# Attention and a ReGLU feed-forward layer on one core: seven products in one more tile, the fourth product ahead of the sixth, later products with v, and merged last stores

## The chip, the core and the metric

The kernel runs on one core of one Trainium2 chip. The core has a matrix engine (TensorE, PE in the profile, with its weight loads shown as PEld), three engines that work on whole tiles (VectorE or DVE, ScalarE or ACT, GpSimd or POOL), a queue engine (SyncE, SP), and 16 DMA engines that they share. The metric is the device time of one execution in microseconds. The kernel before took 361.7 us, the median of three runs (361.11 to 362.02).

## The reference

```
scores = (1/8) * q @ k.T              # 8 batches, 8 heads, 576 rows, head size 64
scores = where(pos//64 >= pos.T//64, scores, -1e9)     # causal by blocks of 64
attn   = softmax(scores) @ v
x      = attn, heads side by side      # 4608 x 512
out    = (relu(x @ w_gate) * (x @ w_val)) @ w_out      # hidden size 1536, out 4608 x 512
```

Inputs and output are float32; the kernel multiplies in bf16 and accumulates in float32.

## The kernel before

**Tiles.** The rows of x are worked through in nine tiles j = 0 to 8 of 512 rows. Tile j < 8 is the first 512 rows of batch j. Tile 8 is made of the last 64 rows of each of the eight batches, the tails. The generator `ffn_gen` (L849) emits the feed-forward work of the tiles in order and yields after each piece, so that other work can be put between. For each tile it first emits 12 pairs of products, gate and val (f = 0 to 11, four 128x512 matmuls each, L855): ACT takes the relu of the gate (L865), DVE multiplies it with val into `hT` (L875). Then comes the product with `w_out`.

**The product with w_out, two ways.** In tiles 0, 1 and 2 it is 48 matmuls of 128x512 (L948), and DVE copies four results out (L958). In tiles from `SEVEN` on (L40, 3 before), `seven_products` (L759) treats each pair of hidden blocks and each half of the columns as a 2x2 block product and forms it from seven products instead of eight: 84 matmuls of 128x256 (L781). This needs sums and differences. Those of the weights are made once: `weight_sums` on POOL (W0 to W5, L684 and L687) and `weight_differences` on DVE, in place in `wo` (D0 to D5, twelve instructions, L698). Those of `hT` are made in each tile by the class `Sums`, twelve DVE instructions (L740): `step(f)` is called while the products of f run, and the last three instructions, `step(12)`, after the last `hT`.

The seven products are taken in the order 5 and 2 (into `y` and `z`), 1, 3 (into `y`), 6, 4 (into `z`), 7. Products 5 and 2 run first over the four hidden pairs that are ready early (`cs=range(4)`) and then over the last two, which need the sums of `step(12)`. Afterwards ACT copies `y` out (L812), DVE adds `z` (L813) and subtracts product 1 (L816); ACT copies `c12` out (L819), POOL makes `c22` (L822), DVE adds product 6 (L825); ACT copies `c21` out (L829), POOL adds it to `g` (L831) and DVE subtracts product 7 (L835; in tile 8 in two halves, L844). Outputs lie in four rotating buffers `ob`. `store_later` (L800) puts off each store until the next one is ready; so the store of a tile's `g` is issued in the next tile, right after its `c12` copy. ACT issues the stores; in tile 8 SP issues half of them.

**Attention rounds.** Beside tile b-1, the kernel does the attention of batch b in four rounds r = 4b to 4b+3 (two heads each). A round has a visit `s` (the products of q and k into a bank `one`, a bank `ffn` and two bank pairs `sc`, and the first exponentials), the last exponential `e`, the corners `c` (memsets of the masked blocks, on DVE at L1008 or POOL at L1011), the products with v of its two heads `a` and `b` (L586, L600, each followed on DVE by a reciprocal, a multiplication and, from batch 3 on, a small third instruction at L532), and `x`, a DMA transpose on SP that brings the rows to `xT` (L635), the operand of the next tile. After the last head of a batch another transpose (L572) brings the tail rows to `xTt`, for tile 8.

**What sets the order.** The order is written out by hand. `AT` (L1105) gives each piece a place on a scale of 144 pieces of feed-forward work per tile; `place_of` shortens the last 48 of them to 42 in tiles of seven products. The loop at its end takes the pieces by place and lets the generator run up to each. Each engine then works through its instructions in this order, waiting by semaphores; nothing overtakes. `HOW` says which engine or PSUM bank a piece uses: for a round, the engine of the corners and the banks of `a` and `b`. From batch 4 on, the last round of a batch uses `sc` for both and the others `one` and `ffn`. PSUM has two `sc` pairs, one `one` and three `ffn` banks; a matmul into a bank waits until its former content has been read.

Of the kernel before, what the change touches and what calls it, by code (L numbers as in the profile page):

```python
# [10 lines left out]
FP = mybir.dt.float32  # L11
BF = mybir.dt.bfloat16
AX = mybir.AluOpType
# [4 lines left out]
def kernel(  # L18
# [10 lines left out]
    nc = tc.nc  # L29

    B, H, S, D = q.shape
# [5 lines left out]


    FIRST = 3
    SEVEN = 3  # L40
    BASE = {0: 0, 1: 512, 3: 896, 2: 1024}
    AW = 1600
    TW = 256
# [9 lines left out]
    psum_ffn = ctx.enter_context(  # L53
        tc.tile_pool(name="psum_ffn", bufs=3, space=bass.MemoryType.PSUM)
    )
# [289 lines left out]
    def dma_transposes(b):  # L345
        m, tl = bfs[b, 0], bfs[b, 1]
        for t in range(2):
            nc.sync.dma_start_transpose(
                (qTm, kTm)[t][b % 2].rearrange("p c h n -> p (c h) n"),
                m[t],  # L350
            )
        tails_by_dma(b, tl)
# [305 lines left out]
    def put_block(j, hi, n0, ob, p0, p1):  # L658

        n = slice(n0, n0 + 256)  # L660
        rows = ob.rearrange("q (p n) -> q p n", n=256)
        if j < B:
            r0 = S * j + 256 * hi + 128 * p0
            nc.scalar.dma_start(
                out[r0 : r0 + 128 * (p1 - p0), n].rearrange("(p q) n -> q p n", q=128),
                rows,
            )
        else:
            for p in range(p0, p1):
                for i in range(2):  # L670
                    r0 = S * (4 * hi + 2 * p + i) + 512
                    (nc.scalar, nc.sync)[i].dma_start(
                        out[r0 : r0 + 64, n], rows[64 * i : 64 * i + 64, p - p0]
                    )

    sevens = []

# [81 lines left out]
    def seven_products(j, quads, sums):  # L759

        def times(to, which, p, c, first):
            two = wo[c // 2][:, 2 * (c % 2) : 2 * (c % 2) + 2, :]  # L770
            t = sevens[c // 2][:, 768 * (c % 2) : 768 * (c % 2) + 768]
            right = {
                5: two[:, 1, 256:512],
                2: two[:, 0, 0:256],
                1: t[:, 0:256],
                3: two[:, 0, 256:512],
                4: two[:, 1, 0:256],
                6: t[:, 256:512],
                7: t[:, 512:768],
            }[which]  # L780
            nc.tensor.matmul(  # L781
                to,
                sums.of(c)[which][:, 128 * p : 128 * p + 128],
                right,
                start=first,
                stop=(c == 5),
                skip_group_check=True,
            )

        def half(to, p):  # L790
            return to[:, 256 * p : 256 * p + 256]

        def whole(to, which, new=True, cs=range(6)):
            for p in range(2):
                for c in cs:
                    times(half(to, p), which, p, c, new and (p, c) == (0, 0))
                    if c % 2:
                        yield

        def store_later(hi, n0, ob, p0=0, p1=2):  # L800
            if store:
                store.pop()()
            store.append(lambda: put_block(j, hi, n0, ob, p0, p1))

        y = psum_ffn.tile([128, 512], FP, name="ffnp")
        z = psum_one.tile([128, 512], FP, name="one")
        for to, which in ((y, 5), (z, 2)):
            yield from whole(to, which, cs=range(4))
        for to, which in ((y, 5), (z, 2)):
            yield from whole(to, which, new=False, cs=(4, 5))  # L810
        g = sb.tile([128, 512], FP, name="ob", bufs=4)
        nc.scalar.copy(g, y)  # L812
        nc.vector.tensor_tensor(out=g, in0=z, in1=g, op=AX.add)  # L813
        m1 = psum_ffn.tile([128, 512], FP, name="ffnp")
        yield from whole(m1, 1)
        nc.vector.tensor_tensor(out=g, in0=m1, in1=g, op=AX.subtract)  # L816
        yield from whole(y, 3, new=False)
        c12 = sb.tile([128, 512], FP, name="ob", bufs=4)
        nc.scalar.copy(c12, y)  # L819
        store_later(0, 256, c12)  # L820
        c22 = sb.tile([128, 512], FP, name="ob", bufs=4)
        nc.gpsimd.tensor_tensor(out=c22, in0=g, in1=c12, op=AX.add)  # L822
        m6 = psum_ffn.tile([128, 512], FP, name="ffnp")
        yield from whole(m6, 6)
        nc.vector.tensor_tensor(out=c22, in0=m6, in1=c22, op=AX.add)  # L825
        store_later(1, 256, c22)
        yield from whole(z, 4, new=False)
        c21 = sb.tile([128, 512], FP, name="ob", bufs=4)
        nc.scalar.copy(c21, z)  # L829
        store_later(1, 0, c21)  # L830
        nc.gpsimd.tensor_tensor(out=g, in0=g, in1=c21, op=AX.add)  # L831
        if j < B:
            m7 = psum_ffn.tile([128, 512], FP, name="ffnp")
            yield from whole(m7, 7)
            nc.vector.tensor_tensor(out=g, in0=g, in1=m7, op=AX.subtract)  # L835
            store_later(0, 0, g)
        else:
            for p in range(2):
                m7 = psum_ffn.tile([128, 512], FP, name="ffnp")[:, 0:256]
                for c in range(6):  # L840
                    times(m7, 7, p, c, c == 0)
                    if c % 2:
                        yield
                nc.vector.tensor_tensor(  # L844
                    out=half(g, p), in0=half(g, p), in1=m7, op=AX.subtract
                )
                store_later(0, 0, half(g, p), p, p + 1)

    def ffn_gen():  # L849
        for j in range(B + 1):  # L850
# [27 lines left out]

            sums = Sums(quads) if j >= SEVEN else None

# [81 lines left out]

            if j >= SEVEN:
                sums.step(12)
# [40 lines left out]
    dve, act, pool = nc.vector.tensor_copy, nc.scalar.copy, nc.gpsimd.tensor_copy  # L1005
# [7 lines left out]
    with tc.manual_schedule(engines={E.PE, E.DVE, E.Activation, E.Pool, E.SP}):  # L1013
# [4 lines left out]
        def round_at(r, how):  # L1018

            exps = []  # L1020

            def begin():
                exps.extend(visit(r))
                exps[0]()
                exps[1]()

            corner, first, second, xT = how
            return {
                f"s{r}": begin,
                f"e{r}": lambda: exps[2](),  # L1030
                f"c{r}": lambda: corners(r, zeros_by[corner]),
                f"a{r}": lambda: head_av(r, 0, first),
                f"b{r}": lambda: head_av(r, 1, second),
                f"x{r}": lambda: (
                    to_xT_pe(r, by[xT[0]], xT[1]) if xT else to_xT_dma(r)
                ),
            }
# [58 lines left out]
        def mains_1(hp):  # L1096
# [8 lines left out]
        AT = {  # L1105
            "Lq0": -63.5,
            "Lq2": -62.27,
            "Lv0": -61.59,
            "Lv2": -59.5,
            "Lq6": -59.5,  # L1110
            "Lq4": -59.5,
            "v00": -58.48,
            "g00": -56.5,
# [214 lines left out]
            "x13": 377.61,  # L1328
            "a14": 378.59,
            "b14": 382.57,  # L1330
            "s15": 383.65,
            "e15": 383.74,
            "x14": 384.44,
            "c15": 388.17,
            "a15": 404.24,
            "b15": 404.37,
            "x15": 406.27,
        }
# [18 lines left out]
            "r11": ("dve", "one", "ffn", None),  # L1357
            "r12": ("dve", "ffn", "sc", None),
            "r13": ("dve", "sc", "ffn", None),
            "r14": ("dve", "sc", "ffn", None),  # L1360
            "r15": ("pool", "ffn", "ffn", None),
            "cv21/1": "dve",
            "cw21/1": "dve",
            "cv00/01": "dve",
# [114 lines left out]
        for b in range(4, B):  # L1479
            base = 144 * (b - 1)  # L1480
            for i in range(4):
                r = 4 * b + i
                here = ("sc", "sc") if i == 3 else ("one", "ffn")
                acts.update(round_at(r, ("dve", *here, None)))
                for n, p in STEADY.items():
                    AT[f"{n}{r}"] = base + 28 * i + p
            acts[f"L{b}"] = lambda b=b: last_keys(b)
            AT[f"L{b}"] = base + 11
            if b + 1 < B:
                acts[f"l{b + 1}"] = lambda b=b: load_qkv(b + 1, (0, 1), products[-1])  # L1490
                acts[f"lv{b + 1}"] = lambda b=b: load_qkv(b + 1, (2,))
                acts[f"d{b + 1}"] = lambda b=b: dma_transposes(b + 1)
                for n, p in (("l", 9), ("lv", 46), ("d", 66)):
                    AT[f"{n}{b + 1}"] = base + p
# [3 lines left out]
        )  # L1498
        for c in range(6):
            AT[f"W{c}"] = 232 + 3 * c  # L1500
            AT[f"D{c}"] = 436 + 5 * c

        assert set(acts) == set(AT), set(acts) ^ set(AT)

        def place_of(p):

            j, o = divmod(p, 144)
            if j < SEVEN:
                return p
            return 144 * SEVEN + 138 * (j - SEVEN) + min(o, 96) + max(0, o - 96) * 42 / 48  # L1510

# [35 lines left out]
```

## Time and profile before

| | |
|---|---|
| median of three runs | 361.7 us (361.11 to 362.02) |
| the profiled execution | 361.8 us |
| its span, first to last instruction | 360.0 us |
| mean granted TensorE clock | 0.997 |
| PE busy | 344.6 us |
| DVE, ACT, POOL busy | 202.5, 178.4, 138.8 us |
| tile 2: products of gate and val | 102 to 130 us |
| tile 2: product with w_out (48 matmuls) | 130.2 to 141.4 us |
| tiles 3 to 8: product with w_out | from 169.0, 206.9, 244.8, 283.9, 315.4 and 345.2 us |
| last matmul starts | 354.2 us |

A timeline line gives the start and the length of an instruction or of a run of equal ones, the engine, the line of the program, what it writes and reads, the shape, the count, and in brackets how long the engine was idle before it and what ended that. Matmul lengths overlap: a 128x512 matmul is listed at 0.38 us, but the next one starts 0.216 us later; a 128x256 one follows after 0.109 us, and one with v after 0.03 us. "ACTq" and "SPq" are the queue parts of those engines, which issue DMAs.

### The profile page before, as it was taken

What the parts mean: (1) busy time and instruction counts of PE and PEld (TensorE: products, weight loads), DVE (VectorE), ACT (ScalarE), POOL (GpSimd) and SP (SyncE); (2) the same over time, 40 slices, a digit from 0 to 9 for tenths busy, and PEclk for the clock granted to TensorE, in tenths of its full rate; (3) what the DMA queues carried; (4) which work ended last, traced back from release to release, by engine and by line L of the source; (5) the groups of instructions that cost most, each with busy time, mean ns of one, the idle gap of its engine ahead of it and who ended that gap; (6) DMA issues with size and microseconds to landing.
All of it is one profiled execution on the core that took longest, in us unless ns stands there. A gap on an engine that the chain in (4) does not pass through costs nothing.

```text
span 360.0 us, 7942 instructions
## 1 busy us (share of the span) xinstructions
PE 344.6 (96%) x3094; PEld 198.8 (55%) x3137; DVE 202.5 (56%) x510; ACT 178.4 (50%) x283; POOL 138.8 (39%) x181
## 2 busy tenths in 40 slices
PE   7899999999999999999999999999899999999993
PEld 3544455545545454555855585557555674484473
DVE  4663445678434454768446754766266745644661
ACT  4933666686336841665166625563555513323320
POOL 4647654697939600770269014830200020011002
PEclk9999999999999999999999999999999999999998
DMA  8999999999999994999479944998500240011005
GB/s 245 296 356 373 316 219 290 194 146 158 193 207 97 158 151 128 80 137 158 109 83 130 152 114 97 129 135 119 131 16 15 17 140 0 0 60 58 2 1 146
DMA packets 155077, 50.00 MB, mean 139 GB/s; under 512 B 134560, under 2 KB 150944, under 8 KB 155040
## 3 DMA queue, kind: packets, MB, share of 16 engines
q0 software_dynamic: 70480, 8.85, 45.5%
q1 hardware_dynamic: 76480, 31.47, 44.4%
q10 hardware_dynamic: 8080, 9.18, 8.2%
q8 instruction: 24, 0.39, 0.5%
q14 instruction: 13, 0.11, 0.1%
HBM read 37.75 MB, written 9.44 MB: 131 GB/s over the span
## 4 chain that ended last, share of the span: by engine, by line
PE 87%; ACT 5%; DVE 4%; issue 2%; POOLq 0%; POOL 0%; DVEq 0%
PE ffnp L855 49%; PE ffnp L781 10%; PE ffnp L948 8%; PE one L781 3%; PE sc L451 3%; PE one L451 2%; PE ffnp L586 2%; ACT attnT L415 2%; PE one L586 2%; ACT attnT L456 2%; PE sc L586 1%; PE one L855 1%; PE one L999 1%; DVE stage L740 1%; DVE hT L875 1%
## 5 line engine op out<-in xcount | busy, mean ns | idle before, releaser
L875 DVE TENSOR_TENSOR hT<-gate_sb,ffnp 128x512 bf16<-128x512 bf16 x106 | 72.6, 685 | 70.4 <-PE ffnp L855 46.1
L855 PE MATMUL ffnp<-xT,wv 128*128 128x512 bf16 x356 | 99.3, 379 | 2.3 <-DVE ob L835 0.7
L865 ACT ACTIVATE gate_sb<-ffnp 128x512 bf16<-128x512 f32 x103 | 62.2, 606 | 76.3 <-PE ffnp L855 71.6
L855 PE MATMUL ffnp<-xT,wg 128*128 128x512 bf16 x348 | 96.7, 380 | 1.3 <-DVE xT L630 0.3
L855 PEld LDWEIGHTS <-wv 128*128 128x128 bf16 x432 | 40.0, 98 | 46.4 <-issue 4.2
L855 PEld LDWEIGHTS <-wg 128*128 128x128 bf16 x432 | 39.7, 98 | 43.1 <-issue 3.1
L822 POOL TENSOR_TENSOR ob<-ob 128x512 f32<-128x512 f32 x6 | 7.6, 1262 | 133.8 <-ACT ob L819 118.5
L456 ACT ACTIVATE attnT<-sc 128x1024 bf16<-128x1024 f32 x56 | 57.3, 1043 | 0.0
L781 PEld LDWEIGHTS <-stage 128*128 128x128 bf16 x360 | 34.7, 98 | 5.2
L586 PEld LDWEIGHTS <-attnT 128*128 128x128 bf16 x640 | 26.3, 98 | 14.6 <-DVE attnT L1008 3.8
L948 PE MATMUL ffnp<-wo,hT 128*128 128x512 bf16 x137 | 33.3, 380 | 0.4
L740 DVE TENSOR_TENSOR stage<-hT 128x512 bf16<-128x512 bf16 (+2 forms) x72 | 33.0, 486 | 0.7
L463 ACT ACTIVATE attnT<-one 128x512 bf16<-128x512 f32 (+1 forms) x28 | 15.0, 536 | 30.5 <-PE ffnp L451 30.5
L339 POOL DMA_DIRECT2D q_bf<-in_q_dram x20 | 17.9, 911 | 27.5 <-DVE hT L875 23.3
L781 PE MATMUL ffnp<-stage 128*128 128x256 bf16 x216 | 26.5, 273 | 0.0
L339 POOL DMA_DIRECT2D v_bf<-in_v_dram x30 | 24.1, 854 | 4.0 <-PE ffnp L855 2.9
L948 PEld LDWEIGHTS <-hT 128*128 128x128 bf16 x144 | 13.3, 98 | 14.0 <-issue 0.6
L451 PEld LDWEIGHTS <-kTm 64*128 64x128 bf16 x384 | 13.1, 94 | 14.3 <-issue 8.3
L339 POOL DMA_DIRECT2D k_bf<-in_k_dram x20 | 17.7, 937 | 0.0
L451 PE MATMUL sc<-qTm,kTm 64*128 64x512 bf16 (+1 forms) x168 | 17.7, 305 | 0.0
L958 DVE COPY ob<-ffnp 128x512 f32<-128x512 f32 x12 | 8.3, 689 | 12.9 <-PE ffnp L948 12.8
L781 PEld LDWEIGHTS <-hT 128*128 128x128 bf16 x144 | 14.1, 98 | 1.6
(143 smaller groups left out, 444.0 us busy)
## 6 DMA issues: line engine op xcount, KB each, us to landing
out_dram<-ob ACTq DMA_DIRECT2D x32, 256.0 KB, 2.8
stage<-in_moe_w_val_dram SPq DMA_DIRECT2D x6, 512.0 KB, 8.2
stage<-in_moe_w_gate_dram SPq DMA_DIRECT2D x6, 512.0 KB, 8.6
stage<-in_moe_w_out_dram SPq DMA_DIRECT2D x6, 512.0 KB, 10.7
q_bf<-in_q_dram POOLq DMA_DIRECT2D x20, 128.0 KB, 4.6
k_bf<-in_k_dram POOLq DMA_DIRECT2D x20, 128.0 KB, 6.5
v_bf<-in_v_dram POOLq DMA_DIRECT2D x20, 128.0 KB, 6.1
stage<-in_v_dram SPq DMA_DIRECT2D x19, 128.0 KB, 5.4
```

Source lines behind the costliest of these rows:

```text
L339: ins = nc.gpsimd.dma_start(dst, part_of)
L451: nc.tensor.matmul(o, kTm[b % 2][head_of(hh), c, hp, :], qT, start=True, stop=True)
L456: return lambda: nc.scalar.activation(at[:, :, lo : lo + 512], sc, AF.Exp, scale=scale)
L463: nc.scalar.activation(at[:, hh, 1024 : 1024 + w], third[hh][:, 0:w], AF.Exp, scale=scale)
L586: nc.tensor.matmul(av[:, p, :], at[:, col : col + 128], v_bf[b % 2][:, c, h, :], start=(p == 0), stop=(c == p), skip_group_check=True,)
L740: nc.vector.tensor_tensor(out=out.rearrange("p (c n) -> p c n", c=m), in0=a, in1=b, op=op)
L781: nc.tensor.matmul(to, sums.of(c)[which][:, 128 * p : 128 * p + 128], right, start=first, stop=(c == 5), skip_group_check=True,)
L855: nc.tensor.matmul(to, (wg, wv)[t][f // 4][:, c, 128 * (f % 4) : 128 * (f % 4) + 128], x[:, c], start=(c == 0), stop=(c == 3),)
L865: nc.scalar.activation(gate_sb, gate, AF.Relu)
L875: nc.vector.tensor_tensor(out=h, in0=gate_sb, in1=val, op=AX.mult)
L948: nc.tensor.matmul(op, hT[f][:, 128 * s : 128 * (s + 1)], wo[f // 4][:, f % 4, n0:n1], start=(f == 0), stop=(f == 11),)
L958: nc.vector.tensor_copy(ob, op)
```

## The change

Five things are edited.

1. `SEVEN` becomes 2: tile 2 uses seven products as well. With it the twelve weight differences move from the start of tile 3 to the start of tile 2, and `place_of` shortens the last part of tile 2.
2. Product 4 is emitted ahead of product 6, with the copy of `c21` and POOL's addition that follow it; the store of `c12` comes behind the `c21` copy on ACT, and the store of `c22` behind that of `c21`.
3. In batches 4 to 7, `a`, `b` and `x` of the last round are put 5 places later.
4. Around tile 2, round 15's visit, exponential and corners come earlier (its visit 12 places), its `a` 4 places earlier. On PE the visit of round 15 now stands ahead of `b13`, `a14` and `b14`, directly behind `a13`. `a14` goes from bank `sc` to `ffn`, `a15` and `b15` from `ffn` to `sc`.
5. In tile 8 each store covers two batches at a time: SP and ACT issue five stores each instead of eight. The last two stay 64 KB each.

```diff
-    SEVEN = 3
+    SEVEN = 2
...
-            for p in range(p0, p1):
-                for i in range(2):
-                    r0 = S * (4 * hi + 2 * p + i) + 512
-                    (nc.scalar, nc.sync)[i].dma_start(
-                        out[r0 : r0 + 64, n], rows[64 * i : 64 * i + 64, p - p0]
-                    )
+            by_batch = out.rearrange("(b s) n -> b s n", b=B)
+            for i in range(2):
+                b0 = 4 * hi + 2 * p0 + i
+                (nc.scalar, nc.sync)[i].dma_start(
+                    by_batch[b0 : b0 + 2 * (p1 - p0) - 1 : 2, 512:576, n].rearrange(
+                        "b s n -> s b n"
+                    ),
+                    rows[64 * i : 64 * i + 64],
+                )
...
-        m6 = psum_ffn.tile([128, 512], FP, name="ffnp")
-        yield from whole(m6, 6)
-        nc.vector.tensor_tensor(out=c22, in0=m6, in1=c22, op=AX.add)
-        store_later(1, 256, c22)
         yield from whole(z, 4, new=False)
         c21 = sb.tile([128, 512], FP, name="ob", bufs=4)
         nc.scalar.copy(c21, z)
         store_later(1, 0, c21)
         nc.gpsimd.tensor_tensor(out=g, in0=g, in1=c21, op=AX.add)
+        m6 = psum_ffn.tile([128, 512], FP, name="ffnp")
+        yield from whole(m6, 6)
+        nc.vector.tensor_tensor(out=c22, in0=m6, in1=c22, op=AX.add)
+        store_later(1, 256, c22)
...
-            "s15": 383.65,
-            "e15": 383.74,
+            "s15": 371.65,
+            "e15": 376.74,
             "x14": 384.44,
-            "c15": 388.17,
-            "a15": 404.24,
+            "c15": 383.17,
+            "a15": 400.24,
...
-            "r14": ("dve", "sc", "ffn", None),
-            "r15": ("pool", "ffn", "ffn", None),
+            "r14": ("dve", "ffn", "ffn", None),
+            "r15": ("pool", "sc", "sc", None),
...
-                    AT[f"{n}{r}"] = base + 28 * i + p
+                    AT[f"{n}{r}"] = base + 28 * i + p + (5 if i == 3 and n in "abx" else 0)
...
-            AT[f"D{c}"] = 436 + 5 * c
+            AT[f"D{c}"] = 293 + 5 * c
```

## The prediction

> **What bounds the kernel.** I read the page first: PE is busy for nearly the whole span, and the chain that ended last lies on it.
>
> ```profile
> span 360.0 us, 7942 instructions
> ...
> PE 344.6 (96%) x3094; PEld 198.8 (55%) x3137; DVE 202.5 (56%) x510; ACT 178.4 (50%) x283; POOL 138.8 (39%) x181
> ...
> PE 87%; ACT 5%; DVE 4%; issue 2%; POOLq 0%; POOL 0%; DVEq 0%
> ```
>
> So a gain is a matmul less, a PE wait less, or a shorter end. After 60 us PE's timeline has waits of over 0.3 us in few places. Four times, in tiles 3 to 6, it waits inside the seven products. Tile 3, by the timeline:
>
> ```profile
> 169.86 1.04 PE L781 MATMUL one<-wo,stage 128*128 128x256 bf16 x8
> 169.97 0.96 DVE L740 TENSOR_TENSOR stage<-hT 128x512 bf16<-128x512 bf16 x3
> 171.02 0.31 DVE L1008 MEMSET attnT<- 64x128 uint32 x2
> 171.24 0.36 PEld L586 LDWEIGHTS <-attnT 128*128 128x128 bf16 x10 [0.63 <-DVE attnT L1008]
> ```
>
> PE has ended the first parts of products 5 and 2 (call this Z, 170.73) and meets `a`, whose corners queue on DVE behind all three sums of `step(12)`: 171.24 - 170.73 = 0.51 us. The second place is the end of tile 5:
>
> ```profile
> 251.68 1.71 ACTq L664 DMA_DIRECT2D out_dram<-ob  x2
> ...
> 255.62 0.58 ACT L829 COPY ob<-one 128x512 f32<-128x512 f32 x1 [3.35 <-PE ffnp L781]
> ...
> 256.25 0.27 PE L451 MATMUL one<-qTm,kTm 64*128 64x256 bf16 x1 [0.25 <-ACT ob L829]
> ...
> 257.63 0.69 DVE L835 TENSOR_TENSOR ob<-ob,ffnp 128x512 f32<-128x512 f32 x1 [3.25 <-PE ffnp L855]
> ...
> 258.37 0.38 PE L855 MATMUL ffnp<-xT,wv 128*128 128x512 bf16 x1 [0.75 <-DVE ob L835]
> ```
>
> The page blames PE for the `c21` copy's wait, but product 4 ended at 254.1. `c21` takes the buffer of the previous tile's `g`, whose store was issued at 251.68 and by the DMA view took 3.8 us to land (2.2 to 2.6 in the five other tiles). In that microsecond a 16 KB instruction fetch (queue q8) lay on a DMA engine. Price: the visit 0.3 late, val 0.9 late, 1.2 us.
>
> **The change, part by part**, on the profiled execution (361.8 us, 0.1 above the median; 1.8 of it lies around the span).
>
> *Tile 2, matmuls.* 48 x 0.216 = 10.37 us go, 84 x 0.1092 = 9.17 come: -1.2. The four DVE copies go and four additions of the same 0.69 us come; ACT gets three copies and POOL two additions, in windows where both idle.
>
> *Tile 2, DVE.* Twelve sums come (0.42 for 512 wide, 0.69 for 1024, 0.29 for 256) and the twelve weight differences, 0.2 apart. The latter find DVE idle between the `hT` of tile 2, and cost nothing; in tile 3, whose products took 0.2 us longer than tile 4's beside them, they are gone: -0.2. The sum after f = 4 falls ahead of the corners of `a12`, which PE awaits already at 114.35: the memsets end 0.34 later: +0.3.
>
> *Round 15's visit* is the costly part. It now comes three matmuls behind `a13`, and its second `sc` pair is the one that `a13` wrote; so it waits for DVE's last reading of `a13`. In the timeline before:
>
> ```profile
> 124.46 0.19 PE L600 MATMUL sc<-v_bf,attnL 128*128 128x65 bf16 x1
> ...
> 124.53 0.63 ACT L865 ACTIVATE gate_sb<-ffnp 128x512 bf16<-128x512 f32 x1
> 124.76 0.31 DVE L1008 MEMSET attnT<- 64x128 uint32 x2 [1.48 <-ACT attnT L456]
> 125.19 0.69 DVE L875 TENSOR_TENSOR hT<-gate_sb,ffnp 128x512 bf16<-128x512 bf16 x1
> 125.80 0.19 DVE L523 RECIPROCAL recip<-sc 128x5 f32<-128x5 f32 x1
> 126.02 0.42 DVE L525 TENSOR_TENSOR xnat<-sc,recip 128x256 bf16<-128x256 f32 x1
> 126.36 0.20 DVE L532 TENSOR_TENSOR xtail<-sc,recip 64x64 bf16<-64x64 f32 x1
> ```
>
> DVE has to do the corners of round 14 (after the exponential that ended at 124.67) and one `hT` (after the relu that ended at 125.16) first, so 126.57 is the earliest as before; a 512-wide sum now stands between them, +0.3: 126.87. PE reaches the pair at 124.49 + 3 x 0.216 + 0.09 + 0.45 (from a visit's start to its second pair, 129.19 to 129.64) = 125.69; with 0.2 from DVE's end to the matmul it starts at 127.1: +1.4 (1.1 without the sum). No bank of the kernel before showed this wait. Behind it queue on PE `b13`, gate and val of f = 10 and 11, `a14`, `b14`; `a14` waits for the `hT` of f = 10 (+0.1), and `b14`, now in the bank ring of `ffn`, for DVE's reading of `a14`, 1.0 us after that one's last matmul, where PE needs 0.9 from there: +0.3 with the load. Round 15's four exponentials on ACT now precede the relus of f = 10 and 11, which still end 0.2 and 0.9 us ahead of their val; its two POOL memsets and SP's transposes have microseconds to spare. The product with w_out then finds its sums: `step(12)`'s first ends 1.7 us after the start, needed at 1.86. Tile 2 together: -1.2 - 0.2 + 0.3 + 1.4 + 0.1 + 0.3 = **+0.7**.
>
> *Later products with v.* At Z PE now runs the last parts of 5 and 2 (0.87 us), which need only the first sum of `step(12)` (170.40), then two matmuls of product 1; `a` starts at Z + 1.09, after the corners (Z + 0.6). Four waits of 0.51 go: **-2.0**. On DVE the addition of `z` now precedes the readings of `a` and `b`; `b`'s ends at Z + 3.65 (before 3.3), and SP's transposes L572 and L635 behind it start at Z + 3.7 and 4.9. The next tile needs the last one at Z + 9.9 (10.4 before); landings there took 2.5 to 4.8, so it just holds.
>
> *Product 4 first.* `c21` could be copied 1.3 us earlier, but its buffer still waits for the `g` store, issued with the `c12` copy and 2.2 to 2.6 us on its way, against 2.8 when product 4 came second. Gain 0.2 to 0.5 of slack and no PE time. The `c12` store moves behind that copy, where ACT stood idle.
>
> *The fetch.* Page and trace give 24 fetches on q8, one per about 256 PE instructions (131 loads with their matmuls). Tile 2 gets 36 pairs more, so every later fetch falls 36 pairs earlier in the work: in tile 5 near Z + 2, ahead of the store: **-1.2**. In tile 6 it moves from Z + 7.9 to about Z + 3.5, onto L572. In tiles 3, 4 and 5 a transpose issue that met a fetch took 1.6 to 2.2 us instead of 1.2 and landed in up to 4.8; by tile 4's rows (2.3 to the next issue, 3.7 to landing) the row for tile 7 lands at Z + 9.7, needed at 9.0: **+0.6**. The Trainium skill ("Runtime: NRT & Kernel Launch", Instruction fetch mechanics) has a boundary of 16 KB cost one mostly hidden DMA step; by that the collision is none of the fetch's doing, the wait of tile 5 would stay, and the sum be 1.2 worse and, without tile 6's, 0.6 better.
>
> *The end.* Now two queues issue 16 stores of 64 KB for 0.5 to 0.6 us each:
>
> ```profile
> 351.21 5.80 SPq L672 DMA_DIRECT2D out_dram<-ob  x8
> ...
> 353.33 4.00 ACTq L672 DMA_DIRECT2D out_dram<-ob  x6
> ```
>
> The `c21` copy waits for tile 7's `g` store until 352.81, so it gains 0.3 (353.22 to 352.9), and the halves of `g` with it. Without the queueing the last issue moves from 356.78 to 356.05: -0.7 at best. Against it: ACT's `c12` half moves from 351.2 to 353.0, so 896 KB go out from 354 on, where now 768 KB took from 354.3 to 358.4, 185 GB/s with the DMA engines 80 to 90% busy: +0.4 at worst. I take **-0.2**, nearest the bandwidth rows. The Trainium skill ("DMA: Bandwidth & Descriptors", Rules for kernel authors) wants small transfers coalesced, and in the same table says that transfers to disjoint partition halves serialize on the same engines. By the first the end would be -0.7; the second stands with the trace.
>
> Sum: 361.8 + 0.7 - 2.0 - 1.2 + 0.6 - 0.2 = 359.7, **359.6 us** from the median.
>
> **Rivals.**
> - *A store or a fetch hits again* (0.20): the 1.2 us of tile 5 stay, or come in another tile. For: one in six tiles was hit; fetches jitter. Against: the moved places. 360.8.
> - *Tile 2 pays in full* (0.12): visit 15 and its followers don't wait. For: PE before had no such wait. Against: the same bank, and DVE's order. 359.6 - 2.1 = 357.5.
> - *Slower: the last transposes come late* (0.12). Each tile's last row block must land within about 4.9 us of its issue (4.0 in tile 6). In the products' stretches landings were 5.6 to 7.3; against it, loads run there, and behind Z none took over 4.8. At 6.0 us: 3 x 1.1 + 2.0, less the 0.6 already counted, is 4.7 more: 364.3. It turns the sign from 5.4 us on.
> - Mine (0.56): 359.6.
>
> **Numbers.** 0.3% (1.1 us) is about what a measurement here can tell from no change. Faster: mine and the full payment, 0.68 to 0.70; same: the second hit and part of the late transposes, 0.18; slower: 0.13. My own case runs from 358.3 (the end's -0.7, visit at 1.1, tile 6 unharmed) to 360.6; the range takes in the rivals next to it: 358.0 to 361.6.
>
> **What the trace after would show.** PE idle before visit 15's second `sc` pair, ended by DVE L532, about 1.4 us; no wait of PE on the corners in tiles 3 to 6; `c21` copies as soon as the `g` store has landed, not at product 4's end; no val late at tile 6's start, the gate of tile 7 on `xT` instead; ten stores at the end and the last matmul near 352.3. I am wrong if tile 3 starts before 141.5, if `a` still waits, or if gates wait for `xT` in tiles 4 to 6.

## The result, and the profile after

The changed kernel takes 359.5 us (median of 13 runs, 358.95 to 361.07), beside 362.85 us for the kernel before (13 runs, 361.04 to 365.8; the three behind the 361.7 us above are the first of them). The ratio is 0.991 (0.988 to 0.994). The profiled execution took 359.73 us, its span is 357.9 us, 2.1 us below that of before.

The page of the changed kernel: PE is still nearly always busy, and one instruction fetch more than before lies in the span (25 on q8, 24 before).

```profile
span 357.9 us, 8015 instructions
...
PE 342.8 (96%) x3131; PEld 202.0 (56%) x3173; DVE 207.5 (58%) x522; ACT 180.1 (50%) x286; POOL 141.2 (39%) x183
...
q8 instruction: 25, 0.41, 0.5%
...
PE 87%; DMA 5%; ACT 3%; POOL 1%; DVE 1%; issue 1%; POOLq 0%; SPq 0%; DVEq 0%; ACTq 0%
```

Lines of the program are three higher from the seven products on (L781 is now L784, L1008 is L1011). In what follows every span is cut into a start and three stretches by the times of PE's matmuls: A from tile 2's first gate matmul to tile 3's, B from there to the start of tile 8's seven products, C from there to the end of the span. Before: 101.86 + 39.60 + 203.70 + 14.85. After: 101.78 + 40.51 + 200.17 + 15.48. So in these two profiles tile 2 cost 0.9 us, the middle gained 3.5, and the end lost 0.6. Of the 0.9, only 0.5 belongs to the program; the rest is a wait that varies from execution to execution, as the experiments show.

**Tile 2.** The timeline after shows the predicted wait of round 15's visit: DVE's memset, sum and `hT` stand ahead of the reading of `a13`, and PE's second `sc` pair waits for L532.

```profile
125.31 0.31 DVE L1011 MEMSET attnT<- 64x128 uint32 x2 [1.49 <-ACT attnT L456]
125.63 0.42 DVE L743 TENSOR_TENSOR stage<-hT 128x512 bf16<-128x512 bf16 x1
...
125.97 0.68 DVE L878 TENSOR_TENSOR hT<-gate_sb,ffnp 128x512 bf16<-128x512 bf16 x1
...
126.02 0.38 PE L451 MATMUL sc<-qTm,kTm 64*128 64x512 bf16 x2
...
126.57 0.19 DVE L523 RECIPROCAL recip<-sc 128x5 f32<-128x5 f32 x1
...
126.79 0.42 DVE L525 TENSOR_TENSOR xnat<-sc,recip 128x256 bf16<-128x256 f32 x1
127.13 0.20 DVE L532 TENSOR_TENSOR xtail<-sc,recip 64x64 bf16<-64x64 f32 x1
...
127.40 0.39 PE L451 MATMUL sc<-qTm,kTm 64*128 64x384 bf16 x4 [0.99 <-DVE xtail L532]
```

**Tiles 3 to 6.** In the timeline of tile 3 PE goes from the first parts of products 5 and 2 into their last parts, then two matmuls of product 1, and `a` starts at 172.43 with no idle time in brackets: the memsets ended 0.5 us earlier.

```profile
171.34 0.60 PE L784 MATMUL ffnp<-wo,stage 128*128 128x256 bf16 x4
171.63 0.31 DVE L1011 MEMSET attnT<- 64x128 uint32 x2
171.78 0.60 PE L784 MATMUL one<-wo,stage 128*128 128x256 bf16 x4
...
172.22 0.38 PE L784 MATMUL ffnp<-stage 128*128 128x256 bf16 x2
...
172.43 0.47 PE L586 MATMUL sc<-v_bf,attnT 128*128 128x65 bf16 x10
```

Apart from single missing records, no gap of PE of over 0.2 us is left from tile 3's start to tile 8's seven products.

**The end.** Here is what I had not seen coming. In the timeline of tile 8 ACT's `c21` copy waits 2.97 us for a DMA:

```profile
347.95 0.59 ACT L822 COPY ob<-ffnp 128x512 f32<-128x512 f32 x1 [2.47 <-PE ffnp L784]
347.96 0.38 ACTq L664 DMA_DIRECT2D out_dram<-ob  x1
348.56 6.54 SPq L672 DMA_DIRECT2D out_dram<-ob  x5
...
351.50 0.58 ACT L828 COPY ob<-one 128x512 f32<-128x512 f32 x1 [2.97 <-DMA out_dram<-ob]
351.52 3.85 ACTq L672 DMA_DIRECT2D out_dram<-ob  x5
```

and the DMA view of 347 to 350 us has the cause: a fetch of 16 KB (at 348.63 in the DMA records) on top of `g`'s store, which took 3.4 us to land (2.2 before).

```profile
q8 instruction: 1, 0.02, 2.7%
issues: line engine op xcount, KB each, median us to landing
out_dram<-ob ACTq DMA_DIRECT2D x1, 256.0 KB, 3.4
```

### The profile page after: what moved, and what is told of

Its sections match the earlier page's. It is cut to its first block, busy times and chain, and to the rows that moved or that the text cites. A ratio compares the mean times of both kernels' runs of the same rounds, so it can differ in the third digit from the quotient of the medians.

```text
span 357.9 us, 8015 instructions
## 1 busy us (share of the span) xinstructions
PE 342.8 (96%) x3131; PEld 202.0 (56%) x3173; DVE 207.5 (58%) x522; ACT 180.1 (50%) x286; POOL 141.2 (39%) x183
## 4 chain that ended last, share of the span: by engine, by line
PE 87%; DMA 5%; ACT 3%; POOL 1%; DVE 1%; issue 1%; POOLq 0%; SPq 0%; DVEq 0%; ACTq 0%
PE ffnp L858 49%; PE ffnp L784 12%; PE ffnp L951 5%; PE one L784 5%; PE sc L451 3%; PE one L451 2%; PE ffnp L586 2%; DMA stage<-in_moe_w_gate_dram 2%; PE one L586 1%; DMA stage<-in_k_dram 1%; PE one L858 1%; PE sc L586 1%; PE ffnp L548 1%; ACT attnT L456 1%; DMA out_dram<-ob 1%
## 5 line engine op out<-in xcount | busy, mean ns | idle before, releaser
L825 POOL TENSOR_TENSOR ob<-ob 128x512 f32<-128x512 f32 x7 | 8.8, 1262 | 142.7 <-ACT ob L822 142.7
L784 PEld LDWEIGHTS <-stage 128*128 128x128 bf16 x420 | 40.4, 98 | 6.0
L743 DVE TENSOR_TENSOR stage<-hT 128x512 bf16<-128x512 bf16 (+2 forms) x84 | 38.5, 485 | 0.9
L784 PE MATMUL ffnp<-stage 128*128 128x256 bf16 x252 | 31.4, 273 | 0.0
L951 PE MATMUL ffnp<-wo,hT 128*128 128x512 bf16 x90 | 22.8, 379 | 0.3
L784 PEld LDWEIGHTS <-hT 128*128 128x128 bf16 x168 | 16.4, 98 | 1.9
L833 DVE TENSOR_TENSOR ob<-ffnp,ob 128x512 f32<-128x512 f32 x7 | 4.8, 692 | 21.6 <-POOL ob L825 15.0
L822 ACT COPY ob<-ffnp 128x512 f32<-128x512 f32 x7 | 4.1, 585 | 21.9 <-PE ffnp L784 21.9
```

What stands on the lines that cost most here:

```text
L743: nc.vector.tensor_tensor(out=out.rearrange("p (c n) -> p c n", c=m), in0=a, in1=b, op=op)
L784: nc.tensor.matmul(to, sums.of(c)[which][:, 128 * p : 128 * p + 128], right, start=first, stop=(c == 5), skip_group_check=True,)
L951: nc.tensor.matmul(op, hT[f][:, 128 * s : 128 * (s + 1)], wo[f // 4][:, f % 4, n0:n1], start=(f == 0), stop=(f == 11),)
```

## The experiments

Twelve kernels, in three groups of four; each group shared its runs of the kernel before (362.4, 362.4 and 362.6 us). Ratios are to those.

| kernel | median us | ratio (95%) | A | B | C |
|---|---|---|---|---|---|
| before | 362.4 to 362.85 | 1 | 39.60 | 203.70 | 14.85 |
| after | 359.5 | 0.991 (0.988-0.994) | 40.51 | 200.17 | 15.48 |
| after_again | 360.2 | 0.993 (0.991-0.996) | 40.74 | 200.16 | 15.59 |
| fetch_moved_after | 359.9 | 0.995 (0.992-0.997) | 41.51 | 200.17 | 14.34 |
| fetch_moved_before | 364.3 | 1.006 (1.004-1.008) | 39.70 | 204.11 | 14.83 |
| visit15_later | 360.0 | 0.994 (0.993-0.996) | 40.41 | 200.17 | 15.62 |
| v_later_alone | 362.0 | 1.000 (0.997-1.002) | 41.10 | 202.72 | 14.82 |
| fetch_tail | 359.15 | 0.990 (0.987-0.993) | 40.12 | 200.22 | 14.27 |
| order_6_4 | 360.3 | 0.995 (0.992-0.998) | 40.71 | 200.17 | 15.20 |
| fetch_tail_16_stores | 360.4 | 0.993 (0.990-0.996) | 40.11 | 200.19 | 15.71 |
| seven_from_tile_3 | 360.1 | 0.992 (0.989-0.995) | 41.35 | 202.17 | 14.28 |
| tails_transposed_later | 366.3 | 1.010 (1.007-1.013) | 47.32 | 200.29 | 15.18 |
| fetch_tail_6_4_in_tile_8 | 359.1 | 0.990 (0.987-0.992) | 40.60 | 200.18 | 14.50 |
| all_together | 365.3 | 1.008 (1.005-1.010) | 48.38 | 200.24 | 14.51 |

A, B and C are of the profiled execution. B repeats to 0.1 us wherever the program of the middle is the same; A does not, and with it the times of equal programs differ by about a microsecond.

What varies in A lies ahead of the last products of q and k of round 12 (L473): near 108 us PE waits for batch 3's transposed q and k, by up to 1.8 us more in one profile than in another. From there to tile 3's first gate, here before and after,

```profile
109.16 0.28 PE L473 MATMUL one<-qTt,kTt 128*128 128x64 bf16 x4
...
141.46 0.59 PE L855 MATMUL ffnp<-xT,wg 128*128 128x512 bf16 x2
```

```profile
109.49 0.28 PE L473 MATMUL one<-qTt,kTt 128*128 128x64 bf16 x4
...
142.29 0.59 PE L858 MATMUL ffnp<-xT,wg 128*128 128x512 bf16 x2
```

it takes 32.25 to 32.30 us in the four profiles whose tile 2 is that of before, and 32.79 to 32.81 in the eight whose tile 2 is that of the changed kernel. So the changed tile 2 costs 0.5 us, in every profile.

### Is it the fetch?

```diff
-            "j0": lambda: junk(7, 512),
+            "j0": lambda: junk(19, 192),
```

In the changed kernel:

> The changed kernel, with the seven 512-wide warm-up matmuls at the start cut into nineteen 192-wide ones: the same columns in a time in which PE waits for its first operands anyway, but twelve loads with twelve matmuls more, so that each later instruction fetch falls twelve pairs earlier in the work. In the changed kernel's profile a fetch at 348.63 us lay on the store of g in tile 8, which took 3.4 us to land instead of the 2.2 of before, and the c21 copy waited for it until 351.50. Fetch theory: the fetch of tile 8 starts 12 x 0.109 = 1.3 us earlier, the store lands in 2.2 to 2.5 us, the c21 copy starts 0.9 to 1.2 us earlier against the last matmul, and the time falls by 0.6 to 1.2 us against the changed kernel (359.5, so 358.3 to 358.9). Rival, the store is slow because SP's store of c12 goes out right behind it: the landing stays at 3.4 us and the time within 0.3 us.

C fell from 15.48 to 14.34 us; `g`'s store, issued at 349.18, let the `c21` copy start at 351.48, 2.3 us later. So the end gained what was expected. But the time did not fall: another fetch (107.10, before that at 109.15) had moved onto the transposes of tile 2. SP's issue of L118 took 2.06 us instead of 1.21, and the visit of round 12 waited 1.24 us for `qTt`:

```profile
105.34 1.18 SPq L117 DMA_TRANSPOSE qTt<-q_bt  x1
...
106.63 2.06 SPq L118 DMA_TRANSPOSE kTt<-k_bt  x1
...
109.40 0.19 PE L451 MATMUL one<-qTt,kTm 64*128 64x64 bf16 x1 [1.24 <-DMA qTt<-q_bt]
```

Other transposes that met a fetch also took 1.6 to 2.2 us to issue. But three profiles have 1.7 to 1.9 us for L117 without a fetch, and v_later_alone and seven_from_tile_3 (below) wait about as long near 108 us without one, so how much of the 1.24 us is the fetch's is not shown.

In the kernel before, with the same edit:

> The kernel before, with the same nineteen narrow warm-up matmuls in place of seven wide ones and nothing else. Fetch theory: the fetch of tile 5 (251.97 us, 0.3 us behind the issue of the store of g) starts about 1.3 us earlier and ends before the store's first packets; the store lands in 2.2 to 2.6 us instead of 3.8, the waits of 0.25 and 0.75 us behind it go, and the time falls by 1.2 us against the kernel before (ratio about 0.9967). The fetch that lay on the transpose in tile 4 costs nothing either way. Rival, the fetch is hidden and the store was late for another cause: the two waits stay and the ratio is 1.000.

The two waits at the end of tile 5 are gone (the store of `g` landed in 2.6 us), as the fetch theory has it. But in tile 6 the fetch, now at 291.00, met the two stores. The second one's issue took 1.73 us, `g`'s landed in 4.0, and the chain is the one that tile 5 had, with one wait of 1.25 us instead of 0.25 and 0.75:

```profile
290.32 2.34 ACTq L664 DMA_DIRECT2D out_dram<-ob  x2
...
294.43 0.59 ACT L829 COPY ob<-one 128x512 f32<-128x512 f32 x1 [3.53 <-PE ffnp L855]
...
295.14 1.26 POOL L831 TENSOR_TENSOR ob<-ob 128x512 f32<-128x512 f32 x1 [2.85 <-ACT ob L829]
...
296.44 0.69 DVE L835 TENSOR_TENSOR ob<-ob,ffnp 128x512 f32<-128x512 f32 x1 [3.42 <-POOL ob L831]
...
297.18 1.02 PE L855 MATMUL ffnp<-xT,wg 128*128 128x512 bf16 x4 [1.25 <-DVE ob L835]
```

The end of tile 5 gained 1.2 us, that of tile 6 lost 1.4 (B +0.4, with 0.2 left over), and the start came 0.4 later. The median rose by 1.9 us, more than these 0.9; what the other runs met is not in this profile and stays open. (Against the first gate of the next tile, the fetches of tiles 5 and 6 came 0.7 and 2.1 us earlier, not the expected 1.3.) In neither kernel was the expected time met; but in both the wait went with the fetch, and in the kernel before it came back where the fetch went.

All fourteen profiles together say when a fetch hurts. They hold 80 stores of a tile's `g` in the next tile. In nine cases a fetch started 0.3 to 0.9 us behind the issue of the store, and these nine landed in 3.1 to 4.0 us. The other 71 landed in 2.1 to 2.6 us, also the twelve at whose issue a fetch was already running. That settles the cause of tile 5's wait and of tile 8's.

### The later products with v alone

```diff
-                    AT[f"{n}{r}"] = base + 28 * i + p
+                    AT[f"{n}{r}"] = base + 28 * i + p + (5 if i == 3 and n in "abx" else 0)
```

> The kernel before with the five places later for a, b and x of the last round of batches 4 to 7, and nothing else. Theory: the four waits for the corners, 0.51 us each, go and nothing comes in their place: 2.0 us faster than the kernel before (ratio about 0.9945), the late val in tile 5 staying, since its fetch stands where it stood. Rival, the transposes behind come too late for the next tile: gates wait for xT in tiles 5 to 8 and the gain is under 1 us.

B fell by 1.0 us only. By tile: the four corner waits are gone (4 x 0.52), tile 5's fetch wait shrank by 0.4, and in tile 6 the gate of tile 7 waits for `xT`. The last transpose of tile 6, issued at 290.36, landed after 5.6 us; the fetch was at 293.97 (the other three tiles: 4.5, 3.6, 4.5). The timeline and the line's own view:

```profile
290.36 1.28 SPq L635 DMA_TRANSPOSE xT<-xnat  x1
...
296.01 0.38 PE L855 MATMUL ffnp<-xT,wg 128*128 128x512 bf16 x1 [1.39 <-DMA xT<-xnat]
```

```profile
DMA to landing us min/median/max: 5.6/5.6/5.6
```

That the fetch made it 1.1 us later than the slowest of the others was not tested by itself. This is my rival of the late last transposes, with a wait of 1.4 to 1.6 us. In the changed kernel the same row lands in 2.5 us (2.8 in tiles 3 to 5).

### Product 4 first

```diff
-        <product 4, c21, store of c21, addition to g>
         <product 6, c22, store of c22>
+        <product 4, c21, store of c21, addition to g>
```

> The changed kernel with product 6 ahead of product 4 again, as before, all else kept. My prediction's step: the order is worth no PE time, since c21 waits for the landing of g's store anyway; the time is within 0.3 us of the changed kernel's. Rival, from the run with only the later products with v, where the c12 store was issued 0.6 us behind that of g and the last row block for tile 7 landed 5.4 us behind its issue: with the order undone, c12's store goes out 2.6 us earlier again, onto the last transposes, which the later products with v have delayed; gates wait for xT in one or more of tiles 4 to 8, 0.5 to 1.6 us each, and the kernel is 1 us slower or more.

B is 200.17 us, as in the changed kernel, and no gate waits for `xT`: the order is worth no PE time there. The rival's mechanism is real, though: with `c12`'s store out earlier the last transposes land in 3.9 to 4.0 us instead of 2.5 to 2.8. In tile 6 the row lands at 293.0, just where tile 7 needs it. The change gives 1.2 us of slack, which no wait in these tiles needed here.

### The end

```diff
-                nc.tensor.matmul(to, <weights>, x[:, c], start=(c == 0), stop=(c == 3))
+                n = 256 if (j, t) == (7, 0) and f < 3 else 512
+                for lo in range(0, 512, n):
+                    nc.tensor.matmul(to[:, lo : lo + n], <weights>, x[:, c, lo : lo + n],
+                                     start=((c, lo) == (0, 0)), stop=(c == 3))
```

> The changed kernel, with the twelve 512-wide gate matmuls of f = 0, 1 and 2 in tile 7 each cut into two of 256 (24 PE instructions more, 12 x 0.002 us of matmul time); so the fetches are where they were up to tile 7 and fall 1.3 us earlier behind it. Moved from the start of the program, the same twelve pairs took the fetch off the store of g in tile 8 (first matmul of its seven products to the end of the span 15.48 -> 14.34 us), but put another one on the transpose L118 in tile 2 (a wait of 1.24 us for qTt). Fetch theory: here tile 2 is as in the changed kernel (tile 3 from about 142.3, no wait for qTt), the stretch from tile 8's seven products to the end is 14.2 to 14.5 us, and the time is 0.9 to 1.2 us below the changed kernel's. Rival: the end is set by the bytes left to store and the stretch stays above 15 us.

C is 14.27 us, 1.2 less than in the changed kernel, and the early part is undisturbed. The store lands in 2.2 us, and the copy waits 1.71:

```profile
350.22 0.59 ACT L828 COPY ob<-one 128x512 f32<-128x512 f32 x1 [1.71 <-DMA out_dram<-ob]
350.25 3.86 ACTq L672 DMA_DIRECT2D out_dram<-ob  x5
```

Its median is 0.4 us below the changed kernel's first measurement and 1.1 below its second, in other groups. Next, the same kernel with the stores of before:

```diff
-            for i in range(2):
-                <one issue over two batches>
+            for p in range(p0, p1):
+                for i in range(2):
+                    <one issue for each batch>
```

> The kernel with the twelve cut gate matmuls in tile 7, and tile 8's stores in sixteen issues of 64 KB again instead of ten. Against the kernel with the cut matmuls and ten stores. If the end is bound by the issues, 0.5 to 0.6 us each on two queues, the stretch from tile 8's seven products to the end is 0.3 to 0.7 us longer. If the 64 KB stores only have slower packets (0.06 us per 1 KB before, against 0.045 with 128 KB), the same sign and about 0.5 us. If the end is bound by the last half of g alone (DVE's second subtraction, then issue and landing), it is equal within 0.15 us.

C is 15.71, so the merged stores are worth 1.44 us in this order of products, more than any of the estimates. From the DMA view of the last stretch (from 8.5 us behind tile 8's seven products to the end; the busy tenths of the DMA engines and the GB/s in 40 slices), first with sixteen stores, then with ten:

```profile
DMA  0006838997998889799899979991196000000000
GB/s 0 0 0 148 188 68 199 228 216 182 205 239 176 199 199 216 171 210 228 182 210 205 222 188 199 216 205 34 23 205 131 6 0 0 0 0 0 0 0 0
```

```profile
DMA  0000179989998899998997888789720000000000
GB/s 0 0 0 0 43 185 199 213 163 235 376 185 163 249 362 348 369 348 206 348 376 249 249 234 284 227 256 235 199 64 0 0 0 0 0 0 0 0 0 0
```

The 185 to 200 GB/s that I had taken for what the DMA engines can do was the rate of a row of 64 KB stores; with 128 KB ones the same engines move up to 376 (the last four stores, of 64 KB, are back at 200 to 280). The engines are about equally busy in both, so the sixteen stores lose by more time for each packet, not by gaps between the issues; why the packets take longer stays open. And the order, in tile 8 alone:

```diff
+        for one_of in (fourth, sixth) if j < B else (sixth, fourth):
+            yield from one_of()
```

> The kernel with the twelve cut gate matmuls in tile 7, with product 6 ahead of product 4 in tile 8 alone. The stretch from tile 8's seven products to the end was 14.27 us with 4 ahead of 6, ten stores and no fetch on the store of g; 15.71 with 4 ahead of 6 and sixteen stores; 14.85 in the kernel before, with 6 ahead of 4 and sixteen stores. If what the order and the number of stores cost adds up, the order costs 0.86 us in tile 8, because ACT's half of c12's store stands behind the c21 copy, which waits for g's store: 14.27 - 0.86 = 13.4 us, and the time falls by 0.9 us against the kernel with the cut matmuls. Rival: with few stores the queues have room, the order is worth nothing at the end, and the stretch is 14.1 to 14.4 us.

C is 14.50, 0.1 us above the rival's range and far from the theory's 13.4: the two costs do not add up. With ten stores product 4 first is even 0.2 us better at the end (14.27 against 14.50; all_together, below, has 14.51 with 6 first); with sixteen it is 0.86 worse (15.71 against 14.85, the latter in the kernel before). So the merged stores are worth 1.44 us with product 4 first, and only 0.35 with product 6 first (14.85 against 14.50). At 359.06 us this is the fastest median of the study, 1.2 us below after_again in the same group, and not told apart from fetch_tail. Both have the shorter end in their profiles; by the intervals of the times alone (0.987 to 0.992 against 0.991 to 0.996) the gain over the changed kernel is likely, not certain.

### The seven products in tile 2

First, with all of tile 2's part undone (`SEVEN = 3`, the differences, places and banks of before):

```diff
-    SEVEN = 2
+    SEVEN = 3
...
-            "s15": 371.65,
+            "s15": 383.65,
...
-            "r14": ("dve", "ffn", "ffn", None),
-            "r15": ("pool", "sc", "sc", None),
+            "r14": ("dve", "sc", "ffn", None),
+            "r15": ("pool", "ffn", "ffn", None),
...
-            AT[f"D{c}"] = 293 + 5 * c
+            AT[f"D{c}"] = 436 + 5 * c
```

> The changed kernel without the seven products in tile 2: SEVEN is 3, the weight differences are back in tile 3, and round 15's visit, corners, a and banks are as before. Theory: tile 3 starts 0.7 to 0.9 us earlier than in the changed kernel and its own stretch is 0.2 us longer, so 0.6 us are gained up to tile 4; but all later fetches move back 36 pairs, onto the store of g in tile 5 (c21's copy and a bank late: 0.8 to 1.2 us of PE waits), while none falls in tile 8 any more (-1.0). In all 0.4 us faster than the changed kernel, within 0.5. Rival, the seven products in tile 2 pay in full and the places of the fetches mean nothing: 1.2 us slower than the changed kernel.

The time is that of the changed kernel within the intervals. B is 2.0 us longer and C 1.2 shorter: the differences back in tile 3 (+0.2), the fetch back on the store of `g` in tile 5 (+1.4, the timeline below), the last row for tile 7 landing in 4.5 us (+0.4), and no fetch in tile 8.

```profile
255.55 0.59 ACT L828 COPY ob<-one 128x512 f32<-128x512 f32 x1 [3.46 <-DMA out_dram<-ob]
...
256.19 0.27 PE L451 MATMUL one<-qTm,kTm 64*128 64x256 bf16 x1 [0.41 <-ACT ob L828]
...
258.31 1.02 PE L858 MATMUL ffnp<-xT,wv 128*128 128x512 bf16 x4 [0.75 <-DVE ob L838]
```

A did not show the expected 0.7 to 0.9: in this execution PE waited for `kTm` and `kTt` near 108 us, as it did in v_later_alone, whose program is that of before up to tile 3. Those two took 41.35 and 41.10 us for A; before itself and fetch_moved_before, with hardly any of these waits, 39.60 and 39.70. So the profile of before that I predicted from was on the lucky side. Behind the waits all four agree, 0.5 us below the changed kernel. The seven products in tile 2 thus cost 0.5 us there and give back 0.2 in tile 3: taken alone they lose 0.3 us. What they gain is the fetch off tile 5's store; what they bring is one onto tile 8's. Then the wait of round 15's visit, taken away by putting it behind `b13`:

```diff
-            "s15": 371.65,
-            "e15": 376.74,
-            "c15": 383.17,
+            "s15": 377.2,
+            "e15": 379.74,
+            "c15": 385.17,
```

> The changed kernel with the visit of round 15 behind b13 and one gate matmul (place 377.2 instead of 371.65; its last exponential at 379.74, its corners at 385.17). Theory of the wait on a13's bank: the second sc pair is now reached at about 128.0 us, after DVE's last reading of a13 (127.34), so the wait of 1.15 us is gone, nothing new waits by more than 0.2 us, and tile 3 starts near 141.2 instead of 142.29: 0.9 to 1.2 us faster than the changed kernel, the fetch in tile 8 being where it was (against the work). Rival, tile 2 is bound by DVE behind it (a14, b14 and the sums of step 12 are late next): tile 3 starts at 142.0 or later and the time falls by 0.3 us at most.

A is 40.41: the rival holds. Behind round 12, tile 2 even takes 33.03 us instead of 32.80. The wait on `a13` is gone, and two others have come, for the bank of f = 10's val, which DVE reads late, and at the seven products' start for ACT's relu of f = 11, behind the visit's exponentials:

```profile
128.53 0.27 PE L451 MATMUL ffnp<-qTm,kTm 64*128 64x256 bf16 x1 [0.77 <-DVE hT L878]
...
132.38 0.82 PE L784 MATMUL ffnp<-wo,stage 128*128 128x256 bf16 x6 [0.33 <-ACT gate_sb L868]
```

### The changed kernel once more, and two attempts to go on

> The changed kernel once more, unchanged, to stand beside the three others on one chip. Expected: 359.5 us, within 0.8 us. The stretch of tile 2 (first gate to tile 3's first gate) has taken 40.1 to 40.7 us in the profiles with its program, of which 0 to 0.5 us is PE waiting for the transposed tails of q and k; the end (tile 8's seven products to the end of the span) 15.2 to 15.5 us, because the fetch falls on the store of g.

360.2 us; A 40.74 and C 15.59, both slightly above what was expected. Next, SP's order in tile 1: the large transposes (L348) of batch 3 earlier.

```diff
-            "d3": 260.7,
+            "d3": 245.0,
+            "d3t": 260.7,
```

> The changed kernel with the two large transposes of batch 3 (L348, 3.6 to 5.0 us of SP each) issued ahead of round 9's transpose instead of behind round 11's; the two small ones for the tails (L117, L118) keep their place. Theory: the waits of PE for qTt and kTt near 108 us (0, 0.2, 0.45, 0.8, 1.2 and 1.7 us in the profiles so far, also in two kernels whose program up to there is that of before) come from SP, which issues L118 only about 1.5 us before it is needed; with L118 3 us earlier they go in every execution. So 0 to 0.5 us faster than the changed kernel in the median, tile 2 at 39.9 to 40.1 us, and a smaller spread. Rival: round 9 to 11's transposes, which now come up to 3 us later, arrive late for tile 2's first gates, and the kernel is up to 2 us slower.

The rival holds, and at nearly three times its price. Beside the loads that still ran, L348 took 6.28 and 7.45 us to issue instead of 4.10 and 3.59 (2.5 to 5.0 in all profiles with its old place); three transposes queue behind it on SP, and tile 2's first gate waits for them:

```profile
87.50 6.28 SPq L348 DMA_TRANSPOSE qTm<-q_bf  x1
...
94.01 7.45 SPq L348 DMA_TRANSPOSE kTm<-k_bf  x1
...
101.56 3.84 SPq L636 DMA_TRANSPOSE xT<-xnat  x3
...
105.12 1.05 PE L859 MATMUL ffnp<-xT,wg 128*128 128x512 bf16 x2 [2.83 <-DMA xT<-xnat]
...
107.85 0.58 PE L859 MATMUL ffnp<-xT,wg 128*128 128x512 bf16 x1 [1.69 <-DMA xT<-xnat]
```

Whether more slack for L118 would steady A was not learnt: L118 came 0.5 us later, not earlier. The last kernel combined this with fetch_tail_6_4_in_tile_8 and

```diff
-            "r14": ("dve", "ffn", "ffn", None),
+            "r14": ("pool", "ffn", "ffn", None),
```

> The changed kernel with the twelve cut gate matmuls in tile 7, product 6 ahead of product 4 in tile 8 alone, batch 3's two large transposes ahead of round 9's, and the corners of round 14 on POOL instead of DVE. The last is the new part: DVE stood idle for 1.49 us with round 14's memset at its head, waiting for ACT's exponential, while the sum and the readings behind it could have run. Theory: with the memset on POOL, DVE's last reading of a13 ends 0.3 us earlier (it is then held by the relu of f = 9), and the wait of round 15's visit falls from 1.15 to about 0.85 us. Sum: -1.2 (fetch), -0.9 or 0 (order), -0.2 (tails), -0.3 (corners): 356.9 to 357.9 us. Rival: POOL's memsets are late for a14, which then waits as long as was saved: tile 2 as in the run without this part.

The loss in tile 2 is the same L348. Its own new part worked as far as it went: the wait of round 15's visit is 0.94 us instead of 1.15 (0.3 was expected), and behind round 12 tile 2 takes 32.59 us instead of 32.80, with C at 14.51.

## Why the prediction was right

The time came where it was predicted, 359.5 for 359.6, but partly by luck. Of the terms two were wrong and nearly cancelled. And the base moved: I had forecast 2.1 us less than 361.7; the kernel before came out at 362.85 in the larger measurement, so that the gain was 3.3 us there, and 2.4 in the second measurement.

- *Tile 2, matmuls, -1.2*: right; the product with w_out takes 10.09 us (132.20 to 142.29) instead of 11.28.
- *The differences gone from tile 3, -0.2*: right, 27.52 to 27.31 us.
- *Waits in tile 2, +2.1 together*: the places right, the sizes a little high. Measured against normal spacing, the visit 1.15 (1.4), `a12` 0.22 (0.3), `a14` 0.12 (0.1), `b14` 0.17 (0.3): 1.7. DVE's order was as written. Its last reading of `a13` ended at 127.33 (predicted 126.87), and PE reached the pair at 126.24 (125.69): all of this came half a microsecond later, PE a little more so, and the wait is shorter by that, and because the matmul came 0.07 us behind DVE's end, not 0.2. With -1.2 for the matmuls A should have grown by 0.5, which is what tile 2 shows behind round 12; the other 0.4 is PE waiting for batch 3's transposes (by the gaps around 108 us, 0.18 for `kTm` and 0.23 for `qTt`, more than in before's profile), which no step of mine had. With the 0.2 of tile 3, the seven products in tile 2 cost 0.3 us instead of the 0.7 of my sum.
- *Later products with v, -2.0*: right, -2.07 (4 x 0.52). The step's last sentence, that the last transposes "just hold", was true here, and in v_later_alone it was not (5.6 us against the 4.0 that I had given as the limit in tile 6).
- *Product 4 first, no PE time*: right (order_6_4). The slack that it gives lies in the last transposes, 1.2 us, which I had not seen.
- *The fetch off tile 5's store, -1.2*: right, -1.22. (The stores of `g` that I compared it with were four, not five.) The Trainium skill ("Runtime: NRT & Kernel Launch", Instruction fetch mechanics) calls the cost mostly hidden. No gap of PE lies at a fetch as such, so far the trace agrees; but a store of `g`, on which PE waits by way of the `c21` copy, landed in 3.1 to 4.0 us instead of 2.1 to 2.6, and that is not hidden.
- *The fetch onto L572 in tile 6, +0.6*: wrong. The fetch was at 287.03 and L572's issue took 1.56 us, but L635 behind it landed in 2.5 us, not at Z + 9.7. I had priced a landing by tile 4's rows, where the stores of `g` and `c12` ran beside it.
- *The end, -0.2*: wrong, +0.6. The term left out the fetch that moving everything by 36 pairs brings into tile 8: +1.21 (fetch_tail). "A store or a fetch hits again", a rival with a price of 1.2 us and a chance of 0.20, came true there; I had counted the fetches up to tile 6 and not through to the end. Without it the end is -0.58 (14.85 to 14.27), within my bounds of -0.7 and +0.4 but near the one that I had set aside: I had read 185 GB/s at 80 to 90% busy as a limit. It is the sum of two effects, each about twice what I had for it: with sixteen stores product 4 first costs 0.86 us, and merging the stores then gains 1.44. The rule of the Trainium skill ("DMA: Bandwidth & Descriptors", Rules for kernel authors) that small transfers be coalesced was the better guide to the sign.

Against the profile of before the terms as measured give 0.9 - 3.5 + 0.6 = -2.0, and without the 0.4 of the transposes -2.4. The medians give -3.3 in the first measurement and -2.4 in the second. The waits near 108 us, which differ by up to 1.8 us between profiles, could make up the rest of the first; that is not shown.

## What to carry to other kernels

An instruction fetch has a place, given to within a microsecond or so by the number of instructions ahead of it; an edit that adds or takes away instructions moved all later ones here. So follow every fetch through to the end of the span and look at what it lands on, before crediting an edit with a wait that came or went; a dozen cut matmuls in the right tile moved one and took 1.2 us off the end of the profile. And when a queue of small stores looks bound by bandwidth, merge them before believing it.

## What was not expected of the hardware

- A 16 KB fetch, mostly 0.9 to 1.5 us long, that starts within a microsecond behind the issue of `g`'s store makes it land in 3.1 to 4.0 us instead of 2.1 to 2.6; one that is already running at the issue does not. Issues that met a fetch took up to 2.2 us on SP instead of 1.2 (three without one reached 1.9), and up to 1.7 on ACT instead of 0.4. A transpose of 5.6 us, instead of 2.5 to 4.5, also shared its time with a fetch.
- The issue of a large transpose (L348) took 2.5 to 5.0 us at its old place in tile 1, and 6.3 to 7.5 where it stood earlier, beside the loads of v. At its old place in tile 2 it took up to 6.5 us as well, so the loads are the likely reason and not a shown one.
- In tails_transposed_later PE ran slowly behind its first wait: the windows of 101 to 105, 105 to 112 and 112 to 120 us show a granted clock of 1.00, 0.51 and 1.00 (columns: busy us of each engine, the clock, DMA share, GB/s).

```profile
101.00:105.00 4.00, 1.28 (x10) 0.53 (x9) 1.09 (x3) 0.00 (x0) 1.42 (x2) 1.00 1.14 174
105.00:112.00 7.00, 5.20 (x27) 2.12 (x27) 1.09 (x3) 1.90 (x3) 0.00 (x0) 0.51 0.46 123
112.00:120.00 8.00, 8.00 (x79) 3.98 (x75) 5.15 (x16) 5.29 (x9) 3.84 (x5) 1.00 0.42 28
```

So two waits of 5 us together (by the starts of the matmuls; 2.83 and 1.69 in brackets) cost about 1.8 us more (A is 6.8 us longer than in the changed kernel). The Trainium skill ("TensorE: Matmul & The Clock Gate", Part 1) has the clock at half after an idle window of about 3.4 us. The first wait was shorter than that, so this run shows the halving and not that figure.
